# A GEGLU feed-forward kernel: up of the first pair of f tiles by seven products too, together with the second pair

## Chip, cores, metric

One core of one Trainium2 chip. The metric is the device time of one execution in microseconds (us). Most executions of one kernel agree to within 0.3%, and all runs quoted here count as fast runs; differences of a few tenths of a per cent are therefore read from ratios with a 95% interval, not from single times.

## The reference

```python
def reference(x, w_gate, w_up, w_down):
    return (_gelu(x @ w_gate) * (x @ w_up)) @ w_down
# x 1 x 2048 x 1024, w_gate and w_up 1024 x 3584, w_down 3584 x 1024, all bf16
```

The 3584 columns of w_gate and w_up are 28 "f tiles" of 128. A pair is two f tiles of both gate and up. The rows of x are worked in two halves of 1024, each of two blocks of 512.

## The kernel before

Nearly every matrix product is done by seven block products in place of eight. For a pair, the four 512 x 128 blocks of a weight are combined into left operands s1, s2, s3, s4 and a22, and the blocks of x into right operands t1, t2, t3, t4 and b22. Two of the seven products use blocks as they are ("direct", bf16), five use prepared operands (f32). A product is four matmuls of 512 columns. The sums are made by three engines: s1, s2, s4 by GpSimd (POOL), t1 to t4 and some s3 by VectorE (DVE), a22 and b22 by ScalarE (ACT).

The chain of dependences matters for all that follows: s2 needs s1, s4 needs s2, t2 needs t1, t4 needs t2; t1 and t3 need the second block of x. The code shown here and below is cut (`...`) and in places drawn together; the comments are added.

```python
def t_sum(name, c0=0, c1=KH):                      # right operands
    ...
    in0, in1 = {
        "t1": lambda: (b(0, 1), b(0, 0)),
        "t2": lambda: (b(1, 1), tsum["t1"].bitcast(F32)[:, c0:c1, :]),
        "t3": lambda: (b(1, 1), b(0, 1)),
        "t4": lambda: (b(1, 0), tsum["t2"].bitcast(F32)[:, c0:c1, :]),
    }[name]()
    dve(nc.vector.tensor_tensor(out=t, in0=in0, in1=in1, op=ALU.subtract))

def s_sum(h, pair, j, name, on_dve=False, staged=True):   # left operands
    ...
    if name == "s1":   tt(a(1, 0), a(1, 1), ALU.add)
    elif name == "s2": tt(s1, a(0, 0), ALU.subtract)      # s1 from above
    elif name == "s3": tt(a(0, 0), a(1, 0), ALU.subtract)
    elif name == "s4": tt(a(0, 1), s2, ALU.subtract)      # s2 from above
    else:              act(nc.scalar.copy(out=t, in_=a(1, 1)))
```

Only the first pair of the program is not done so, since at the start there is no time to prepare operands: it is 64 direct matmuls, during which the rest is loaded and the second pair's operands are made.

```python
def first_pair_units(hT):
    held = (VB, RB)
    transpose_x0(0)
    warm(RB[1], TB // 2)
    part(held, 0, 0, KPQ, js=(0,))      # gate, first block of x
    transpose_x0(1)
    part(held, 0, 0, KPQ, js=(1,))      # up
    part(held, 0, KPQ, KD)              # gate and up, the rest of the first block
    t_sum("t1", 0, KH // 2)
    t_sum("t1", KH // 2, KH)
    ...
    held = (QB, PB)
    part(held, 1, 0, KH)                # gate and up, second block of x
    t_sum("t2")
    t_sum("b22")
    t_sum("t3", 0, KH // 2)
    ...
    for name in ("s1", "s2", "s4"):     # operands of the second pair
        for j in range(2):
            s_sum(0, 1, j, name)
```

The loads ahead of it bring only the first 256 columns (two f tiles) of the first 512 of gate and up. The other 256 of both follow behind the second block of x.

```python
FA = 2 * P
load_x0(0, sp, 0, 2)
load_x0(0, act, 2, TSB)
load_w(first, 0, 0, 2, sp, 0, FA)
load_x0(1, act)
load_w(first, 1, 0, 2, sp, 0, FA)
load_w(first, 0, 2, 5, act, 0, FA)
load_w(first, 1, 2, 5, sp, 0, FA)
...                                     # transposed x of the first block, weights 5 to 8
for k0, k1 in ((0, 2), (2, KH), (KH, KD)):
    load_xT(xT, 0, 1, k0, k1)           # second block of x
for j in range(2):
    load_w(first, j, 0, KD, sp, FA, FG) # late columns of gate and up
```

Of the kernel before, what the change touches and what calls it, by code (L numbers as in the profile page):

```python
# [34 lines left out]
def kernel(  # L35
# [8 lines left out]
    nc = tc.nc  # L44
# [77 lines left out]
    def act(inst):  # L122
        return on("act", inst)

    def dve(inst):
        return on("dve", inst)
# [55 lines left out]
        new_x(tb)  # L182
    new_chunk((0, 0))

    FA = 2 * P
    first = (0, 0)
    load_x0(0, sp, 0, 2)
    load_x0(0, act, 2, TSB)
    load_w(first, 0, 0, 2, sp, 0, FA)
    load_x0(1, act)  # L190
    load_w(first, 1, 0, 2, sp, 0, FA)
    load_w(first, 0, 2, 5, act, 0, FA)
    load_w(first, 1, 2, 5, sp, 0, FA)
    ident = const_pool.tile([P, P], BF16, name="ident")
    make_identity(nc, ident[:])

# [13 lines left out]

    for i in range(NWARM):
        warm(i)

    load_xT(xT, 0, 0, KH, KH + 1)
    behind_transpose = last_on["sp"]
    load_xT(xT, 0, 0, KH + 1, KH + 2)
    for j in range(2):
        load_w(first, j, 5, KD, act, 0, FA)
        tc.add_manual_dep(
            last_on["act"].ins,  # L220
            behind_transpose.ins.name,
            SCHED_DEP,
            reason="engine order",
        )
    act(nc.scalar.preload_act_table(ACT.Gelu_apprx_tanh))
    load_xT(xT, 0, 0, KH + 2, KD)
    for k0, k1 in ((0, 2), (2, KH), (KH, KD)):
        load_xT(xT, 0, 1, k0, k1)
    for j in range(2):
        load_w(first, j, 0, KD, sp, FA, FG)  # L230
    new_chunk((0, 1))
    for j in range(2):
        load_w((0, 1), j, 0, KD)


    tsum = {}
# [35 lines left out]

    g_ctr = [0]

    def gelu(ps, last=False):

        if last:
            g_sb = o_pool.tile([P, TB], F32, name="o_sb")[:]
        else:
            e0 = 4 * CH + (g_ctr[0] % 4) * 2 * TB  # L280
            g_ctr[0] += 1
            g_sb = w_mem[:, e0 : e0 + 2 * TB].bitcast(F32)
        act(nc.scalar.activation(out=g_sb, in_=ps[:], func=ACT.Gelu_apprx_tanh))  # L283
        return g_sb

    def mult(hT, g_sb, ps, fc, tb):
        dve(
# [5 lines left out]
            )  # L293
        )

    def unit_out(hT, bset, fi, tb):
        mult(hT, gelu(banks[bset[0]]), banks[bset[1]], fi, tb)

    def transpose_x0(q):

        parts = [(2 * q, 0, 4), (2 * q + 1, 0, 4)]
        if q == 0:
            parts = [(0, 0, 2), (0, 2, 4), (1, 0, 4)]
        for n, (kd, ts0, ts1) in enumerate(parts):
            tp = banks[(PB + QB)[(2 * q + n) % 4]][:].bitcast(BF16)
            for ts in range(ts0, ts1):
                pe(
                    nc.tensor.transpose(  # L308
                        tp[:, ts * P : (ts + 1) * P],
                        xs0[:, ts, kd * P : (kd + 1) * P],  # L310
                        ident[:],
                    )
                )
            cols = slice(ts0 * P, ts1 * P)
            if q == 0 or n == 0:
                dve(nc.vector.tensor_copy(out=xT[0][:, kd, cols], in_=tp[:, cols]))
            else:
                act(nc.scalar.copy(out=xT[0][:, kd, cols], in_=tp[:, cols]))

    def part(held, tb, k0, k1, us=(0, 1), js=(0, 1)):  # L320
        for kd in range(k0, k1):
            for j in js:
                for u in us:
                    mm_gu(banks[held[u][j]], chunks[first][j], u, tb, kd)

    def first_pair_units(hT):

        held = (VB, RB)
        transpose_x0(0)
        warm(RB[1], TB // 2)  # L330
        part(held, 0, 0, KPQ, js=(0,))
        transpose_x0(1)
        part(held, 0, 0, KPQ, js=(1,))
        part(held, 0, KPQ, KD)
        t_sum("t1", 0, KH // 2)
        t_sum("t1", KH // 2, KH)
        for u in range(2):
            unit_out(hT, held[u], u, 0)
        held = (QB, PB)
        part(held, 1, 0, KH)  # L340
        t_sum("t2")
        t_sum("b22")
        t_sum("t3", 0, KH // 2)
        part(held, 1, KH, KD, (0,))
        unit_out(hT, held[0], 0, 1)
        t_sum("t3", KH // 2, KH)
        part(held, 1, KH, KD, (1,))
        unit_out(hT, held[1], 1, 1)
        for j in range(2):
            s_sum(0, 1, j, "s3", True, False)  # L350
        for name in ("s1", "s2", "s4"):
            for j in range(2):
                s_sum(0, 1, j, name)


    ssum = {}
# [1 line left out]

    def block(key, j, i, kh):
        fi = 2 * (key[2] % PPG) + i  # L360
        w_sb = chunks[(key[0], key[2] // PPG)][j]
        return w_sb[:, half(kh), fi * P : (fi + 1) * P]

    def s_sum(h, pair, j, name, on_dve=False, staged=True):
        key = (h, "p", pair)

        def a(i, kh):
            return block(key, j, i, kh)

        if on_dve and staged and name in ("s1", "s2", "s3"):  # L370

            if j == 0:
                first_s[name] = wd_pool.tile([P, WDT, D], BF16, name="wd_sb")
            t = first_s[name][:, j, :].bitcast(F32R)
        else:
            s0 = (2 * S_NAMES.index(name) + j) * KH * P
            t = s_mem[:, s0 : s0 + KH * P]
        t = t.rearrange("p (a b) -> p a b", b=P)
        ssum[(h, pair, j, name)] = t

        def tt(in0, in1, op):
            if on_dve:
                dve(nc.vector.tensor_tensor(out=t, in0=in0, in1=in1, op=op))
            else:
                pool(nc.gpsimd.tensor_tensor(out=t, in0=in0, in1=in1, op=op))  # L385

        if name == "s1":
            tt(a(1, 0), a(1, 1), ALU.add)
        elif name == "s2":
            s1 = ssum[(h, pair, j, "s1")].bitcast(F32)  # L390
            tt(s1, a(0, 0), ALU.subtract)
        elif name == "s3":
            tt(a(0, 0), a(1, 0), ALU.subtract)
        elif name == "s4":
            s2 = ssum[(h, pair, j, "s2")].bitcast(F32)
            tt(a(0, 1), s2, ALU.subtract)
        else:
            act(nc.scalar.copy(out=t, in_=a(1, 1)))  # L398
# [6 lines left out]
    def pair_quads(hT, h, pair, nxt, then):  # L405
# [49 lines left out]
        def do_m5(j):  # L455
            mm(V_[j], j, s(j, "s1"), tsum["t1"], True)
            m5[j] = m_pool.tile([P, TB], F32, name=f"m5_{j}")
            act(nc.scalar.copy(out=m5[j][:], in_=banks[V_[j]][:]))  # L458
            if not eager:
                prep(j, "s1")  # L460

        def do_m6(j):
            mm(QB[j], j, s(j, "s2"), tsum["t2"], False)
# [3 lines left out]
            mm(P_[j], j, block(key, j, 0, 0), b11, True)  # L467
            act(nc.scalar.copy(out=banks[QB[j]][:], in_=banks[P_[j]][:]))  # L468
        behind = len(pending) > 0
        eager = not behind and "m2" in then  # L470
        if behind:

            pending.pop()()
# [1 line left out]
        if behind:  # L475
            if nxt is None:
                m2()
                done("m2")
            else:
                pending.append(m2)  # L480
            order = (do_m6, 0), (do_m6, 1), (do_m5, 0), (do_m5, 1)
        elif eager:
            m2()
            done("m2")
            order = (do_m5, 0), (do_m5, 1), (do_m6, 0), (do_m6, 1)
        else:
            pending.append(m2)
            order = (do_m5, 0), (do_m6, 0), (do_m6, 1), (do_m5, 1)
# [3 lines left out]
                done("m6")  # L492
        for j in range(2):
            add_m5(QB[j], QB[j])
            if not eager:
                prep(j, "s2")
        done("m5")
        if eager:
            pool_behind_dve()
            for name in ("s1", "s2"):  # L500
                for j in range(2):
                    prep(j, name)
        for j in range(2):
            mm(RB[j], j, s(j, "s3"), tsum["t3"], False)
            add_m5(V_[j], RB[j])
# [343 lines left out]
    for h in range(NH):  # L849
        hT = hT_pool.tile([P, KF, SH], BF16, name="hT")  # L850
        first_pair = 0
        if h == 0:
            first_pair_units(hT)
            first_pair = 1
            xs = [(tb, kd) for tb in (1, 0) for kd in range(KD)]
            new_x(1)
            stage_load(0)
            stage_load(1)
        for pair in range(first_pair, NPAIR):
            then = {}  # L860
            if pair % PPG == 0 and (pair // PPG + 1) * PPG < NPAIR:
                key = (h, pair // PPG + 1)

                if key not in chunks:
                    new_chunk(key)
                    for j, at in enumerate(("m2 of last", "m3")):
                        then[at] = [lambda j=j: load_w(key, j, 0, KD, act)]
            if h == 0 and pair < PPG:
                then = {
                    "m2": [lambda j=j: s_sum(0, pair, j, "a22") for j in range(2)]  # L870
                    + [lambda: t_sum("t4", 0, KH // 2)],
                    "m5": [lambda: t_sum("t4", KH // 2, KH)],
                }
            if h == 0 and pair >= PPG:

                n = [min(4 * (pair - PPG + d), NSTEP) for d in range(3)]
                steps = [lambda k=k: stage_step(k) for k in range(n[0], n[1])]
                new = range((n[1] + 2) // 3, (n[2] + 2) // 3)

# [53 lines left out]
        if h + 1 < NH:  # L933
# [1 line left out]
            new_x(0)  # L935

            def x_fill():
                for k0, k1 in ((0, 2), (2, KH), (KH, KD)):
                    src = x_rows(k0, k1)
                    sp(nc.sync.dma_start(out=xT[0][:, k0:k1, :], in_=src))  # L940

# [66 lines left out]
```

## Time and profile before

| | before |
|---|---|
| median of the runs beside the change | 540.12 us (539.45 to 541.44, 6 runs) |
| TensorE (PE) busy | 99% of the span |
| waits of PE | one, 0.8 us, at the very start |
| third pair begins on PE | 32.09 us |
| late columns of up landed (POOL's first sum of them) | 19.07 us |

The kernel is bound by PE from beginning to end, so what matters is whether PE ever stands still. The mark used throughout is the moment at which the third pair begins on PE: from there on both kernels do the same, and what is behind at this mark is behind at the end, give or take a wait of up to 1.1 us just behind it. The table of stretches shows what the other engines do meanwhile. Its columns are: stretch in us, its length, then busy us and instructions of PE, weight loads, DVE, ACT and POOL, the granted clock of PE, the mean busy share of the DMA engines and what they moved in GB/s.

```profile
18.00:23.00 5.00, 4.95 (x24) 2.36 (x24) 5.00 (x5) 2.79 (x6) 4.62 (x4) 1.00 1.10 343
23.00:28.00 5.00, 5.00 (x24) 3.90 (x23) 5.00 (x6) 3.17 (x6) 5.00 (x3) 1.00 0.85 296
```

From 18 to 28 us DVE and POOL are both busy nearly all the time, that is working or standing in each other's way, and the DMA still moves about 300 GB/s. PE is fully busy nevertheless: until 22.71 us it does direct products, which need none of what DVE and POOL are making, and by then the first prepared operands are there.

### The profile page before, as it was taken

How to read it: one execution, taken by the hardware profiler on the slowest of the kernel's cores; microseconds unless marked ns; L12 is line 12 of the kernel's file. 1: busy time of each engine (PE TensorE's matmuls, PEld its weight loads, DVE VectorE, ACT ScalarE, POOL GpSimd, SP SyncE). 2: the span in 40 equal slices, each digit the busy share in tenths (PEclk: the TensorE clock that was granted, in tenths of full speed). 3: DMA queues.
4: the chain of work that ended last, by engine and by line, in shares of the span. 5: the costliest groups of instructions: out<-in, count | busy, mean ns of one | idle time of the engine just before them, and what ended most of it. 6: DMA issues, size and time to landing. Idle time of an engine off the chain costs nothing.

```text
span 537.8 us, 7068 instructions
## 1 busy us (share of the span) xinstructions
PE 531.9 (99%) x2348; PEld 377.9 (70%) x2384; DVE 363.9 (68%) x475; ACT 263.2 (49%) x446; POOL 244.3 (45%) x212
## 2 busy tenths in 40 slices
PE   9999999999999999999999999999999999999997
PEld 4577777667776686777776677777777766866866
DVE  2988767788775997989674334444454469969961
ACT  2555555555555329117465555555555551452270
POOL 0689877777776000000066766667777730000000
PEclk9999999999999999999999999999999999999999
DMA  9946876685816977779940404042222447677846
GB/s 215 328 120 194 213 242 209 221 266 187 292 60 207 356 237 265 230 271 318 321 161 1 156 1 158 24 134 71 86 78 80 157 143 282 228 230 252 292 146 207
DMA packets 92419, 102.70 MB, mean 191 GB/s; under 512 B 18656, under 2 KB 67296, under 8 KB 92384
## 3 DMA queue, kind: packets, MB, share of 16 engines
q1 hardware_dynamic: 69584, 80.30, 45.8%
q10 hardware_dynamic: 22800, 21.96, 13.1%
q8 instruction: 19, 0.31, 0.3%
q14 instruction: 16, 0.13, 0.1%
HBM read 85.98 MB, written 12.58 MB: 183 GB/s over the span
## 4 chain that ended last, share of the span: by engine, by line
PE 99%; issue 0%; ACT 0%; ACTq 0%
PE bank L413 63%; PE bank L700 33%; PE bank L264 3%; PE bank L202 1%; PE bank L308 0%; ACT o_sb L753 0%; ACT bank L468 0%; ACTq L753 0%; ACTq L468 0%
## 5 line engine op out<-in xcount | busy, mean ns | idle before, releaser
L413 PE MATMUL bank<-t_mem,s_mem 128*128 128x512 f32 x1056 | 249.4, 394 | 0.0
L413 PEld LDWEIGHTS bank<-t_mem,s_mem 128*128 128x128 f32 x1056 | 198.1, 188 | 43.8 <-ACT bank L464 0.3
L385 POOL TENSOR_TENSOR s_mem<-w_mem 128x512 fp32r<-128x512 bf16 x102 | 119.4, 1192 | 190.3 <-DMA w_mem<-in_w_up_dram 103.1
L700 PE MATMUL bank<-t_mem,s_mem 128*128 128x512 f32 x544 | 127.1, 392 | 0.0
L288 DVE TENSOR_TENSOR hT<-w_mem,bank 128x512 bf16<-128x512 f32 x104 | 71.2, 686 | 80.5 <-PE bank L413 46.2
L700 PEld LDWEIGHTS bank<-t_mem,s_mem 128*128 128x128 f32 x544 | 102.2, 188 | 22.1
L436 DVE TENSOR_TENSOR bank<-bank,m 128x512 f32<-128x512 f32 x108 | 69.8, 694 | 44.6 <-ACT m L458 43.3
L413 PE MATMUL bank<-xT,w_mem 128*128 128x512 bf16 x405 | 96.5, 380 | 1.4
L283 ACT ACTIVATE w_mem<-bank 128x512 f32<-128x512 f32 x104 | 61.8, 596 | 53.1 <-DVE bank L436 35.6
L413 PEld LDWEIGHTS <-w_mem 128*128 128x128 bf16 x432 | 40.2, 98 | 51.6 <-issue 6.8
L385 POOL TENSOR_TENSOR s_mem<-w_mem,s_mem 128x512 fp32r<-128x512 bf16 x52 | 66.4, 1301 | 0.0
L605 DVE TENSOR_TENSOR t_mem<-w_mem 128x1024 fp32r<-128x1024 bf16 x56 | 65.6, 1218 | 0.0
L385 POOL TENSOR_TENSOR s_mem<-s_mem,w_mem 128x512 fp32r<-128x512 f32 x52 | 61.3, 1199 | 0.0
L464 ACT COPY bank<-bank 128x512 f32<-128x512 f32 x54 | 30.8, 570 | 38.9 <-PE bank L413 38.9
L398 ACT CAST s_mem<-w_mem 128x512 fp32r<-128x512 bf16 x54 | 33.1, 615 | 30.6 <-PE bank L413 29.1
L675 DVE TENSOR_TENSOR s_mem<-hT 128x512 fp32r<-128x512 bf16 x52 | 34.2, 686 | 10.0 <-PE bank L700 9.4
L458 ACT COPY m<-bank 128x512 f32<-128x512 f32 x54 | 31.7, 587 | 17.5 <-PE bank L413 17.5
L700 PEld LDWEIGHTS <-hT 128*128 128x128 bf16 x224 | 21.3, 98 | 26.6 <-issue 2.1
L468 ACT COPY bank<-bank 128x512 f32<-128x512 f32 x54 | 30.7, 570 | 12.7 <-PE bank L413 12.7
L753 ACT CAST o_sb<-bank 128x512 bf16<-128x512 f32 x28 | 15.4, 586 | 39.6 <-PE bank L700 39.6
L630 DVE TENSOR_TENSOR o_sb<-wd_sb,o_sb 128x512 fp32r<-128x512 bf16 x28 | 31.5, 1126 | 0.5
L602 ACT CAST t_mem<-w_mem 128x1024 fp32r<-128x1024 bf16 x28 | 26.9, 1048 | 0.0
(42 smaller groups left out, 237.9 us busy)
## 6 DMA issues: line engine op xcount, KB each, us to landing
t_mem<-t_dram SPq DMA_DIRECT2D x56, 512.0 KB, 5.3
w_mem<-in_w_gate_dram ACTq DMA_DIRECT2D x10, 1024.0 KB, 5.1
w_mem<-in_w_up_dram ACTq DMA_DIRECT2D x10, 1024.0 KB, 5.4
wd_sb<-in_w_down_dram SPq DMA_DIRECT2D x28, 256.0 KB, 4.2
t_dram<-o_sb SPq DMA_DIRECT2D x28, 256.0 KB, 2.4
wd_sb<-in_w_down_dram SPq DMA_DIRECT2D x12, 512.0 KB, 7.8
w_mem<-in_w_down_dram SPq DMA_DIRECT2D x4, 1024.0 KB, 6.3
w_mem<-in_w_down_dram SPq DMA_DIRECT2D x8, 512.0 KB, 8.6
```

What stands on the lines that cost most here:

```text
L283: act(nc.scalar.activation(out=g_sb, in_=ps[:], func=ACT.Gelu_apprx_tanh))
L288: nc.vector.tensor_tensor(out=hT[:, fc, tb * TB : (tb + 1) * TB], in0=g_sb, in1=ps[:], op=ALU.mult,)
L385: pool(nc.gpsimd.tensor_tensor(out=t, in0=in0, in1=in1, op=op))
L398: act(nc.scalar.copy(out=t, in_=a(1, 1)))
L413: nc.tensor.matmul(banks[bank][:], lhsT=lhs[:, c, :], rhs=rhs[:, c, :], start=start and c == 0, stop=c == KH - 1, skip_group_check=True,)
L436: nc.vector.tensor_tensor(out=banks[dst][:], in0=banks[src][:], in1=m5[j][:], op=ALU.add)
L458: act(nc.scalar.copy(out=m5[j][:], in_=banks[V_[j]][:]))
L464: act(nc.scalar.copy(out=banks[RB[j]][:], in_=banks[QB[j]][:]))
L605: dve(nc.vector.tensor_tensor(out=t, in0=in0, in1=in1, op=ALU.subtract))
L630: dve(nc.vector.tensor_tensor(out=t, in0=in0, in1=in1, op=ALU.subtract))
L675: dve(nc.vector.tensor_tensor(out=t, in0=in0, in1=in1, op=op))
L700: nc.tensor.matmul(banks[bset[u]][:], lhsT=lhs(i, u), rhs=rhs(i), start=start and i == 0, stop=stop and i == NS - 1, skip_group_check=True,)
```

## The change

The intent: the up half of the first pair is also done by seven products, which saves 4 of its 32 matmuls. It is done in one run with the second pair, as three "units": gate of the second pair, up of the first, up of the second. Gate of the first pair stays direct.

The pairs of the first chunk become f tiles (0, 2) and (1, 3). The direct gate then needs tiles 0 and 2, so all of gate's columns have to come early, in rows of 1024 bytes; of up only two tiles are early, and its late columns are needed by both up units. They are queued behind the second block of x. The head's loads are also cut into smaller pieces, spread over two queues. Cut to its core:

```diff
-    FA = 2 * P
-    load_x0(0, sp, 0, 2)
-    load_x0(0, act, 2, TSB)
-    load_w(first, 0, 0, 2, sp, 0, FA)
     ... (the rest of the loads shown above)
+    def head_w(j, k0, k1, queue):
+        load_w(first, j, k0, k1, queue, 0, (FG, 2 * P)[j])   # gate whole, up half
+    head(head_x, sp, 0, 0)
+    head(head_x, act, 0, 2)
+    head(head_w, sp, 0, 0, 1)
+    head(head_w, act, 0, 1, 2)
     ... (nine more pieces of x, gate, up and transposed x)
+    head(head_w, act, 1, KH, KD)
+    head(head_xT, sp, 0, KH + 2, KD)
+    head(head_w, act, 0, KH + 2, KD)
+    for k0, k1 in ((0, 2), (2, KH), (KH, KD)):
+        head(head_xT, sp, 1, k0, k1)
+    load_w(first, 1, 0, KD, sp, 2 * P, FG)                   # late columns of up
-    def first_pair_units(hT):
     ...
+    def first_chunk(hT):
+        units = ((1, 0), (0, 1), (1, 1))                     # (pair, 0 gate / 1 up)
     ...
+        gate(0, KD - 2, KD)
+        s(0, "a22")
     ...
+        for name in ("s1", "s2", "s4"):
+            s(0, name)
+        t_sum("t1", 0, KH // 2)
+        t_sum("t1", KH // 2, KH)
+        for name in ("s1", "s2", "s4"):
+            for i in each[1:]:
+                s(i, name)
+        for i in each:
+            on_x0(i, KD - 2, KD)
+            unit_out(i, banks[P_[i]], 0, 0)
+        gate(1, 0, KD)
+        t_sum("t2")
+        t_sum("b22")
+        for i in each[1:]:
+            t_sum("t3", (i - 1) * KH // 2, i * KH // 2)
+            s(i, "s3", True)
+        gate_out(1)
+        for i in each:
+            product(i, P_[i], "s1", "t1", True)
+            copy(m5[i], P_[i])
     ...
+        for i in each:
+            product(i, Q_[i], "s2", "t2")
+            copy(banks[R_[i]], Q_[i])
+        add(banks[Q_[0]], Q_[0], 0)
+        t_sum("t4", 0, KH // 2)
     ... (s3, s4, a22 with t3, b22, t4 in the same way)
 def block(key, j, i, kh):
     fi = 2 * (key[2] % PPG) + i
+    if (key[0], key[2] // PPG) == first:
+        fi = key[2] + 2 * i
 ...
             def x_fill():
-                for k0, k1 in ((0, 2), (2, KH), (KH, KD)):
+                for k0, k1 in ((0, KD),):
```

The marked cuts also hide the removal of a special order for the second pair (`eager`) that is no longer needed.

## The prediction

> **What bounds the kernel now.** I read the page first, then the matmul groups by form, the waits of the tensor engine, and the timeline of the first 45 us, because the change touches only the first chunk of weights (f tiles 0 to 3) and the loads ahead of it.
>
> ```profile
> PE 531.9 (99%) x2348; PEld 377.9 (70%) x2384; DVE 363.9 (68%) x475; ACT 263.2 (49%) x446; POOL 244.3 (45%) x212
> PE 99%; issue 0%; ACT 0%; ACTq 0%
> ```
>
> The tensor engine is busy 99% of the span and is 99% of the chain that ended last. The waits of PE hold a single entry:
>
> ```profile
> PE bank L202 <- PEq L992: 0.8, 1, 0.8
> ```
>
> So in this kernel one matmul saved is one matmul's pace saved, and any wait put on PE is added to the end in full, since nothing behind it has slack to take it up. Two rules of pace come from the timeline of PE:
>
> ```profile
> 6.49 13.11 PE L264 MATMUL bank<-xT,w_mem 128*128 128x512 bf16 x59
> 19.43 3.63 PE L413 MATMUL bank<-xT,w_mem 128*128 128x512 bf16 x15
> 22.71 9.54 PE L413 MATMUL bank<-t_mem,s_mem 128*128 128x512 f32 x40
> 32.09 1.90 PE L413 MATMUL bank<-xT,w_mem 128*128 128x512 bf16 x7
> 33.64 9.44 PE L413 MATMUL bank<-t_mem,s_mem 128*128 128x512 f32 x40
> 42.93 3.63 PE L413 MATMUL bank<-xT,w_mem 128*128 128x512 bf16 x15
> ```
>
> The reader is to see the starts: 6.49 to 19.43 us is 60 bf16 matmuls of the first pair (one record missing), 0.216 us each. From 33.64 to 42.93 us is 40 f32 ones, 9.29 us; single records inside it stand 0.2275 us apart, apart from the first. The chunk ends, for this argument, where the third pair begins: 32.09 us. That is the mark to beat.
>
> **What the Trainium skill says.** "TensorE: Matmul & The Clock Gate", section "Back-to-back issue gap", gives N/2.4 + 2.5 ns when warm, 215.8 ns for N = 512; the trace agrees for bf16 (0.216). The f32 step of 0.2275 is a little more. "SBUF — State Buffer", section "SBUF: two separate sides", says that VectorE with two SBUF inputs and GpSimd share a port pair held as "an exclusive lock, not a bandwidth split"; the loser waits for the whole instruction. The trace agrees to a few hundredths of a us:
>
> ```profile
> 15.40 2.29 DVE L259 TENSOR_TENSOR t_mem<-xT,t_mem 128x2048 fp32r<-128x2048 bf16 x1
> 17.60 2.18 DVE L259 TENSOR_TENSOR t_mem<-xT 128x1024 fp32r<-128x1024 bf16 x1
> 20.30 1.58 DVE L259 TENSOR_TENSOR t_mem<-xT 128x1024 fp32r<-128x1024 bf16 x1
> ...
> 17.34 1.35 POOL L385 TENSOR_TENSOR s_mem<-w_mem 128x512 fp32r<-128x512 bf16 x1 [16.04 <-DMA w_mem<-in_w_gate_dram]
> 19.07 1.72 POOL L385 TENSOR_TENSOR s_mem<-w_mem 128x512 fp32r<-128x512 bf16 x1 [0.38 <-DMA w_mem<-in_w_up_dram]
> 20.76 3.71 POOL L385 TENSOR_TENSOR s_mem<-s_mem,w_mem 128x512 fp32r<-128x512 f32 x2
> ```
>
> POOL's first sum ends at 18.69; the DVE difference issued at 17.60 ends at 19.78, 1.09 us later; POOL's second ends at 20.79, 1.01 us later; DVE's next ends at 21.88, 1.09 later. They alternate. So I take 1.05 us of the port for a POOL sum, 1.09 for a DVE difference of 1024 columns, 2.29 for one of 2048, and 0.52 for a DVE weight sum of 512 (two took 22.40 to 25.02 with two POOL turns between). "DMA: Bandwidth & Descriptors", section "Latency and other measured facts", gives 261 GB/s for DMA transposes; here the stretch from 8 to 13 us, nearly all transposes, moved 232, while 18 to 23 us (rows of 1024 bytes) moved 343.
>
> **The change part by part.**
>
> 1. Matmuls. Up of the first pair goes from 32 direct matmuls to 28 (two direct products of 4, five of prepared operands of 4). Over the program the instruction order has 24 fewer bf16 matmuls and 20 more f32 ones: 24 x 0.216 - 20 x 0.2275 = 5.18 - 4.55 = 0.63 us off. If nothing waits, the time is 539.97 - 0.63 = 539.3. Everything else decides by how much this is overdrawn.
>
> 2. Order on PE. Before: 64 direct matmuls, then the second pair (16 direct, 40 prepared). After: 40 direct on the first block of x, 16 gate on the second block, then 60 prepared in the order s1, s2, s3, s4, a22, three units each. With PE starting as before, the prepared ones start 8 x 0.216 earlier than 19.43: 17.7 us. Each product of 4 takes 0.91: s1 of the units at 17.7, 18.6, 19.5; s2 at 20.4, 21.3, 22.3; end at 31.4 without waits (32.09 - 31.4 is the 0.63 again, give or take rounding). Before, the prepared products began at 22.71, five us later.
>
> 3. Loads. Units two and three are the up halves, pairs of f tiles (0,2) and (1,3), so both need the late columns of up. These are queued behind x of the second block. In the kernel before, POOL's second sum tells when the late up landed: 19.07. By then 4.0 MB had landed: x 0.5, early weights 1.0, transposed x 1.5, late gate and late up 1.0. After, the same 4.0 MB lie in front of the same landing, because all of gate now comes first. Gate in rows of 1024 bytes and fewer stretches of bare transposes save perhaps half a us: late up at 18.5 (estimate; 17.8 to 19.2). X of the second block, last at 15.06 before, has 0.5 MB more ahead of it: about 16.4.
>
> 4. The port. POOL needs four sums after 18.5 (s1, s1, s2, s2) before PE's sixth product, which without waits would start at 22.3. Alone they would take 4 x 1.05 and end at 22.7. But DVE holds the same port in turn: t1 (two of 1.15), two products off PSUM (0.68 each), t2 (2.29), t3 in halves (1.09), s3 of the units (0.52). POOL also makes s1, s2, s4 of the gate unit from about 12.3 on, when gate has landed, and these take turns with t1, whose inputs land at 13.3 and 14.5. Running it by hand: t1 is done at 17.2, s4 of the gate unit at 18.3, the first s1 of up at 19.5 (or behind t2, at 20.8), t2 at 21.7, the second s1 at 22.8, half of t3 23.9, s2 25.0, s3 25.5, the last s2 26.5. The sixth product then starts at 26.6 and not 22.3. Nine products follow, 8.2 us, after its own 0.9: end at 35.7, if DVE's adds and t4 keep up; they come out within 1 us of the limit on either side. Against 32.09 this is 3.6 later, up to 4.9 where t4 and the adds bind too.
>
> 5. The rest. Two sums of the following pair are made behind t4 as before; the single load of transposed x for the second half replaces three far ahead of use. I give both 0.
>
> The head may lose 0 to 0.5 us on late gate or up rows (needed near 10.7 and 12.2, landing near 10.5 and 12), but that is hidden: the end of the chunk hangs on the port chain. Sum: 539.97 + 3.6 to 4.9 by my central run; a run in which all lands as early as before gives about +1.5. I take +3.8: **543.8 us**.
>
> **The rivals.** *First: no new wait.* The author placed the loads and sums with care, and the saving of 0.63 would show: 539.3. For it speaks that PE waits nowhere now, in a head just as tight. Against it: the prepared products come 5 us earlier than before while the late columns they rest on come no more than half a us earlier or so. *Second: the wait is only that for late up* (POOL and DVE don't collide much): the last s2 at 23 to 24, +0.5 to +1.5, so 540.5 to 541.5. Against it speaks the alternation in the lines above. *Third: the head stalls too or PE's clock drops in the waits.* The waits come in pieces of about a us; the clock column shows 9 in all slices. A drop to half pace over some us would add 1 to 2: 545 to 546. *Fourth: DVE alone binds* through t2, t3, the adds and t4 (9.6 us of its own work after t2 starts near 18): +1 to +4.9, about what the port gives.
>
> **Range and chances.** None of these is near 2% (10.8 us). The low end allows for the second rival: 540.2. The high end takes the port with DVE's adds: 545.6. First rival about 1 in 8. Faster by 2% has no mechanism: 0.002; slower by 2% would need 12 us of wait: 0.013.
>
> **What would show it.** In the profile after: x24 fewer bf16 and x20 more f32 matmuls on PE; waits of PE on POOL's sums (s_mem) or gaps before the prepared products between 18 and 28 us, of 3 to 5 us in all; POOL's first sum of up starting at 18 to 19.5 us behind a DMA of up; sums of 1.5 to 2.3 us in turns with DVE; the third pair beginning near 35.5 instead of 32.09. If POOL's last s2 is done by 22.3 us, or PE has no gap there, I am wrong, and the time is 539.3. If late up lands before 17 us, step 3 is wrong; if sums and differences overlap freely, step 4 is.

## The result, and the profile after

A ratio is the mean time of one kernel's fast runs over that of the other's of the same rounds, so it isn't quite the ratio of the medians.

| | before | after |
|---|---|---|
| median | 540.12 us | 545.75 us (545.2 to 547.78, 6 runs) |
| ratio | | 1.0107 [1.0088, 1.0127] |
| third pair begins on PE (profiled run) | 32.09 us | 39.64 us |
| PE's prepared products begin | 22.71 us | 19.81 us |
| t4 complete | 29.5 us | 34.1 us |

The change costs about 5.6 us. It is the same at a threshold of 2%, but clearly not a gain. The profiled execution of the changed kernel was the slowest of its six (547.78 us), which matters below. Two lines of the page:

```profile
PEclk9889999999999999999999999999999999999999
PE 94%; DMA 2%; POOL 2%; issue 1%; SPq 0%; ACT 0%; POOLq 0%; ACTq 0%
```

The chain that ended last was PE for 99% before; now DMA and POOL have 2% each of it. The clock line shows 8 in the second and third slice (13.6 us each). The waits of PE (us in total, times, longest), without the 0.8 us at the start that it had before:

```profile
PE bank L386 <- POOL s_mem L519: 2.6, 2, 1.9
PE bank L271 <- DMA xT<-in_x_dram: 1.7, 3, 0.8
PE bank L359 <- DMA w_mem<-in_w_up_dram: 0.2, 1, 0.2
```

Before, that one was the only wait: now PE also waits for POOL's sums and for loads. The timeline of PE (start, duration, instruction, in brackets the idle time before it and what ended it) shows where:

```profile
18.27 1.89 PE L271 MATMUL bank<-xT,w_mem 128*128 128x512 bf16 x8 [0.64 <-DMA xT<-in_x_dram]
19.81 1.28 PE L386 MATMUL bank<-t_mem,s_mem 128*128 128x512 f32 x4
22.97 1.35 PE L386 MATMUL bank<-t_mem,s_mem 128*128 128x512 f32 x4 [1.88 <-POOL s_mem L519]
25.06 12.92 PE L386 MATMUL bank<-t_mem,s_mem 128*128 128x512 f32 x44 [0.74 <-POOL s_mem L519]
...
39.64 1.90 PE L547 MATMUL bank<-xT,w_mem 128*128 128x512 bf16 x7
```

One product is done, then PE waits 1.88 us for s1 of the second unit and 0.74 for that of the third. After 25.06 the list shows 44 matmuls without a gap, yet 12.92 us for them; at 0.2275 us each they would take 10. The table of stretches tells why:

```profile
18.00:23.00 5.00, 2.85 (x13) 1.47 (x12) 5.00 (x5) 3.63 (x7) 2.29 (x2) 1.00 1.08 328
23.00:28.00 5.00, 4.25 (x11) 3.00 (x12) 5.00 (x4) 1.41 (x3) 5.00 (x3) 0.59 1.08 365
28.00:33.00 5.00, 5.00 (x17) 3.95 (x17) 4.36 (x6) 2.50 (x5) 4.40 (x3) 0.73 0.07 23
```

PE does 13, 11 and 17 matmuls where it did 24 in each of these stretches before, and its granted clock falls to 0.59 and 0.73: the clock records have half speed from 23.89 to 30.71 us. In that time the matmuls stand 427 ns apart. So two causes lie on top of each other in this trace, waits for sums and a slow clock, and the trace alone can't say which of them carries the 5.6 us. DVE meanwhile is as full as before, and POOL's first sum of up waits for a load. Its timeline, with DVE's between:

```profile
12.94 1.15 POOL L519 TENSOR_TENSOR s_mem<-w_mem 128x512 fp32r<-128x512 bf16 x1 [11.63 <-DMA w_mem<-in_w_gate_dram]
...
20.71 4.29 POOL L519 TENSOR_TENSOR s_mem<-w_mem 128x512 fp32r<-128x512 bf16 x2 [3.29 <-DMA w_mem<-in_w_up_dram]
24.97 3.72 POOL L519 TENSOR_TENSOR s_mem<-s_mem,w_mem 128x512 fp32r<-128x512 f32 x2
```

```profile
21.83 2.17 DVE L266 TENSOR_TENSOR t_mem<-xT 128x1024 fp32r<-128x1024 bf16 x1
23.92 1.64 DVE L517 TENSOR_TENSOR s_mem<-w_mem 128x512 fp32r<-128x512 bf16 x1
```

A POOL sum with nobody beside it takes 1.15 us. The four of up take about 2 us each, and each difference of DVE beside them about 1 us more than alone (1.21 and 0.68, as an experiment below shows): they take turns. The last s2 is done at 28.69, and after it DVE has all of t4 still to make. The landings themselves stand in the trace too: the last piece of x of the second block landed at 18.23 us (15.06 before), the late columns of up at 20.64 (19.01 before).

### The profile page after: what moved, and what is told of

Read it like the earlier page. It is cut to its first block, busy times and chain, and to the rows that moved or that the text cites. A ratio compares the mean times of both kernels' runs of the same rounds, so it can differ in the third digit from the quotient of the medians.

```text
span 545.7 us, 7082 instructions
## 1 busy us (share of the span) xinstructions
PE 535.1 (98%) x2345; PEld 380.4 (70%) x2380; DVE 367.6 (67%) x479; ACT 264.7 (49%) x449; POOL 248.5 (46%) x215
## 3 DMA queue, kind: packets, MB, share of 16 engines
q10 hardware_dynamic: 22832, 22.42, 13.6%
## 4 chain that ended last, share of the span: by engine, by line
PE 94%; DMA 2%; POOL 2%; issue 1%; SPq 0%; ACT 0%; POOLq 0%; ACTq 0%
PE bank L547 60%; PE bank L822 32%; PE bank L386 3%; POOL s_mem L519 2%; DMA w_mem<-in_w_gate_dram 1%; DMA w_mem<-in_w_up_dram 1%; SPq L166 0%; ACT o_sb L875 0%; SPq L160 0%; POOLq L519 0%; ACTq L875 0%
## 5 line engine op out<-in xcount | busy, mean ns | idle before, releaser
L547 PE MATMUL bank<-t_mem,s_mem 128*128 128x512 f32 x1016 | 239.8, 394 | 0.0
L547 PEld LDWEIGHTS bank<-t_mem,s_mem 128*128 128x128 f32 x1016 | 190.8, 188 | 41.8
L822 PE MATMUL bank<-t_mem,s_mem 128*128 128x512 f32 x544 | 127.4, 393 | 0.0
L301 DVE TENSOR_TENSOR hT<-w_mem,bank 128x512 bf16<-128x512 f32 x100 | 68.6, 686 | 79.8 <-PE bank L547 45.6
L822 PEld LDWEIGHTS bank<-t_mem,s_mem 128*128 128x128 f32 x544 | 102.1, 188 | 22.5 <-DVE s_mem L797 0.4
L570 DVE TENSOR_TENSOR bank<-bank,m 128x512 f32<-128x512 f32 x104 | 67.3, 694 | 46.5 <-ACT m L592 45.0
L547 PE MATMUL bank<-xT,w_mem 128*128 128x512 bf16 x390 | 92.9, 380 | 1.4
L283 ACT ACTIVATE w_mem<-bank 128x512 f32<-128x512 f32 x100 | 59.5, 597 | 44.8 <-DVE bank L570 32.7
L547 PEld LDWEIGHTS <-w_mem 128*128 128x128 bf16 x416 | 38.6, 98 | 49.7 <-issue 6.8
L519 POOL TENSOR_TENSOR s_mem<-w_mem,s_mem 128x512 fp32r<-128x512 bf16 x53 | 68.4, 1314 | 0.1
L532 ACT CAST s_mem<-w_mem 128x512 fp32r<-128x512 bf16 x54 | 33.2, 615 | 33.8 <-PE bank L547 29.5
L597 ACT COPY bank<-bank 128x512 f32<-128x512 f32 x52 | 29.6, 570 | 38.2 <-PE bank L547 38.2
L822 PEld LDWEIGHTS <-hT 128*128 128x128 bf16 x224 | 21.3, 98 | 26.6 <-issue 2.1
L592 ACT COPY m<-bank 128x512 f32<-128x512 f32 x52 | 30.6, 589 | 17.0 <-PE bank L547 17.0
L601 ACT COPY bank<-bank 128x512 f32<-128x512 f32 x52 | 29.7, 570 | 11.7 <-PE bank L547 11.7
L752 DVE TENSOR_TENSOR o_sb<-wd_sb,o_sb 128x512 fp32r<-128x512 bf16 x28 | 29.5, 1052 | 0.5
```

Of the source, the lines that this page charges most:

```text
L283: act(nc.scalar.activation(out=g_sb, in_=ps[:], func=ACT.Gelu_apprx_tanh))
L301: nc.vector.tensor_tensor(out=hT[:, fc, tb * TB : (tb + 1) * TB], in0=g_sb, in1=ps[:], op=ALU.mult,)
L519: pool(nc.gpsimd.tensor_tensor(out=t, in0=in0, in1=in1, op=op))
L547: nc.tensor.matmul(banks[bank][:], lhsT=lhs[:, c, :], rhs=rhs[:, c, :], start=start and c == 0, stop=c == KH - 1, skip_group_check=True,)
L570: nc.vector.tensor_tensor(out=banks[dst][:], in0=banks[src][:], in1=m5[j][:], op=ALU.add)
L592: act(nc.scalar.copy(out=m5[j][:], in_=banks[V_[j]][:]))
```

## The experiments

My theory: the operands of the prepared products can't exist when PE gets to them, because the sums of POOL and of DVE share one port and start only when the late loads land; the products were to come 5 us earlier (they came 2.9 us earlier in the trace) and the operands didn't. Rivals: the slow clock is the cause; the landing of up's late columns alone is; the rearranged loads are. Each kernel ran in rounds beside the kernel before. The experiments ran in three groups of four, each group on one chip; the kernel before had medians of 540.23, 540.19 and 540.23 us beside them.

### The same kernel again

No edit. It separates the slow clock of a single execution from what belongs to the kernel.

> The changed kernel, unaltered, for a second trace and its spread. Expected 545 to 546.5 us. The first trace had four kinds of loss before the third pair: waits for loads in the head (2.6 us), waits for POOL's sums of up (3.1 us), half clock from 23.9 to 30.7 us (about 2.7 us), against 0.63 saved. If these are regular, they show again, and the third pair begins at 37.5 to 40 us (32.1 in the kernel before). If the stretch of slow loads at 7 to 12 us was a chance of that one execution, the head's waits are gone here and the time still stays near 545.5, because POOL's chain sets the end.

Measured: 546.92 us (545.46 to 547.13), ratio 1.0113 [1.0097, 1.013]; third pair at 39.27 us; half clock again in the profiled run (mean 0.994). The result repeats. But of the first six executions two had a mean clock of 1.000 and took 545.39 and 546.11 us, amid the four others, whose clock was 0.994 to 0.997 and whose times were 545.2 to 547.78. So the slow clock comes in some executions only, and the loss is there without it. (The 2.6 us of waits for loads in the expectation are too many: the waits shown above add up to 1.9.)

### PE kept busy in the waits

Matmuls on constants, into a bank that the next product overwrites, fill the two waits.

```diff
         for i in each:
+            for _ in range((0, 7, 4)[i]):
+                warm(P_[i])
             product(i, P_[i], "s1", "t1", True)
```

> Dummy matmuls fill the two waits for POOL's sums: 7 before s1 of the second unit, 4 before s1 of the third, into the bank that the next product clears. Theory (the half clock is the tensor engine's answer to its waits): clock 1.0 throughout, no matmuls of 427 ns between 20 and 35 us, time 0.5 to 2.7 us below the changed kernel of the same rounds (some of its executions had no half clock or a short one). Rival (the clock falls for other reasons, or POOL's chain is later anyway and hides it): no gain, or half clock all the same.

Measured: 545.95 us (545.35 to 546.27), ratio 1.0103 [1.0088, 1.0118], clock 1.0 throughout. The timeline of PE:

```profile
28.29 7.59 PE L386 MATMUL bank<-t_mem,s_mem 128*128 128x512 f32 x32 [0.67 <-POOL s_mem L521]
...
37.53 1.90 PE L549 MATMUL bank<-xT,w_mem 128*128 128x512 bf16 x7
39.86 7.52 PE L549 MATMUL bank<-t_mem,s_mem 128*128 128x512 f32 x32 [0.42 <-DVE hT L301]
```

At full clock PE gets to the sixth product sooner and waits there for POOL's s2; it goes on at 28.29 us, ends 1.7 to 2.1 us sooner than in the two traces with the slow clock, and then waits 0.42 us for DVE inside the third pair. The median is 0.97 us below that of the repeat beside it, which the theory's 0.5 to 2.7 includes, but 0.2 above that of the first six executions, and the intervals of the ratios overlap. So the slow clock is real and may be up to 2 us of the slowest executions, but for the most part it fills time in which PE would have waited for operands: at full clock 5.7 us are still lost. It is not the cause.

### No sums of up on POOL (wrong result on purpose)

The two up units use gate's s1, s2 and s4 in place of their own, so that POOL has six sums fewer. The loads, DVE's work and PE's matmuls stay.

```diff
         for name in ("s1", "s2", "s4"):
             for i in each[1:]:
-                s(i, name)
+                pair, j = units[i]
+                ssum[(0, pair, j, name)] = ssum[(0, 1, 0, name)]
```

> Wrong result on purpose: units two and three (up) use the gate unit's s1, s2 and s4 in place of their own, so POOL makes three sums in the first chunk and not nine, and these products wait neither for POOL nor for the late up columns (s3 and a22 of up still do). Theory (POOL's sums behind the late landing set the end): PE has no wait for POOL, third pair begins at 33 to 35 us, time 540.5 to 542.5. Rival (head and the vector engine's t2, t3, adds and t4 set it anyway): 544 or more.

Measured: 541.09 us (540.84 to 542.04), ratio 1.0018 [1.0003, 1.0033]. PE and DVE:

```profile
19.06 12.17 PE L386 MATMUL bank<-t_mem,s_mem 128*128 128x512 f32 x52
...
32.88 1.90 PE L548 MATMUL bank<-xT,w_mem 128*128 128x512 bf16 x7
35.40 9.33 PE L548 MATMUL bank<-t_mem,s_mem 128*128 128x512 f32 x40 [0.61 <-DVE hT L301]
```

```profile
21.14 1.21 DVE L266 TENSOR_TENSOR t_mem<-xT 128x1024 fp32r<-128x1024 bf16 x1
22.28 0.68 DVE L518 TENSOR_TENSOR s_mem<-w_mem 128x512 fp32r<-128x512 bf16 x1
```

All waits between the products are gone, and the time falls by 5.8 us against the unchanged repeat on the same chip, by 4.9 against keep_warm, which like it ran at full clock. DVE's instructions take 1.21 and 0.68 us where they took 2.17 and 1.64, and t4 is complete at 28.8 us in place of 34. So POOL's sums of up carry the loss. But this edit takes away two things at once: the work on the port, and the wait for the late columns, which these sums need. The next two take them apart.

### The up units on columns that are there early (wrong result on purpose)

```diff
         if (key[0], key[2] // PPG) == first:
-            fi = key[2] + 2 * i
+            fi = key[2] + 2 * i if j == 0 else (key[2] + i) % 2
```

Up's operands are made from f tiles 0 and 1, which land early; all work stays.

> Wrong result on purpose: the up units take all their blocks from the early columns, so nothing waits for the late ones; POOL makes all its nine sums, and these still share with the vector engine. Theory A (the late landing is what hurts): near no_up_sums, 541 to 542.5. Theory B (the turns with the vector engine hurt even with columns early): POOL runs from 13 us without a pause, six sums and three with turns of about 1.05 plus the differences, last s2 of up near 22 to 24 us, 543 to 544.5.

Measured: 546.8 us (546.46 to 547.0), ratio 1.012 [1.0105, 1.0135], clock 1.0. No gain, and above both ranges: it is even 0.85 us slower than keep_warm, which ran at full clock too. POOL, then PE:

```profile
18.84 4.31 POOL L519 TENSOR_TENSOR s_mem<-w_mem 128x512 fp32r<-128x512 bf16 x2
23.11 3.71 POOL L519 TENSOR_TENSOR s_mem<-s_mem,w_mem 128x512 fp32r<-128x512 f32 x2
```

```profile
23.20 3.30 PE L386 MATMUL bank<-t_mem,s_mem 128*128 128x512 f32 x12 [1.94 <-POOL s_mem L519]
26.88 4.85 PE L386 MATMUL bank<-t_mem,s_mem 128*128 128x512 f32 x20 [0.38 <-POOL s_mem L519]
32.35 2.08 PE L386 MATMUL bank<-t_mem,s_mem 128*128 128x512 f32 x8 [0.62 <-DVE bank L409]
...
37.56 1.90 PE L547 MATMUL bank<-xT,w_mem 128*128 128x512 bf16 x7
40.55 6.63 PE L547 MATMUL bank<-t_mem,s_mem 128*128 128x512 f32 x28 [1.10 <-DVE hT L301]
```

POOL waits for no load between its sums and is through with s2 at 26.8 us, 1.3 to 1.9 sooner than in the three traces with up's own columns. PE still waits 2.3 us for its sums. And in exchange POOL's turns delay DVE's t2 (3.17 us where it took 2.28), so PE now also waits 0.62 and 0.15 for DVE's adds and 1.10 for DVE's product in the third pair, and t4 isn't complete before 33.9. The landing of the late columns isn't what the end hangs on. The second block of x, from which DVE's chain starts, landed late in this run as well (17.48 us); no run moved that alone.

### The sums of up on DVE

s1 and s2 of the up units go from POOL to DVE, behind t2; s4 stays with POOL. The result is correct.

```diff
-        for name in ("s1", "s2", "s4"):
-            for i in each[1:]:
-                s(i, name)
 ...
         t_sum("t2")
+        for name in ("s1", "s2"):
+            for i in each[1:]:
+                s(i, name, True)
+        for i in each[1:]:
+            s(i, "s4")
```

> The up units' s1 and s2 (four sums) are made on the vector engine behind t2 and not on POOL; s4 stays on POOL. Correct result. No_up_sums and early_cols say that the turns of POOL and the vector engine on one port set the end, not the late landing. If it is the turns, four turns of 1.05 us and the alternation go for four vector sums of 0.55 to 0.7, all in one queue: s1 of the second unit ready near 22, s2 of the third near 24, PE's third pair at 35 to 36.5 and the time 542 to 543.5. If the sheer amount of work on the vector engine binds, no gain: 545 to 547.

Measured: 545.91 us (545.53 to 546.52), ratio 1.0105 [1.009, 1.012]; third pair at 37.65 us. The second alternative came true, no gain. The waits of PE:

```profile
PE bank L271 <- DMA xT<-in_x_dram: 2.0, 2, 1.2
PE bank L386 <- DVE t_mem L266: 1.3, 1, 1.3
PE bank L549 <- DVE hT L301: 1.1, 1, 1.1
PE bank L386 <- DVE s_mem L519: 1.0, 1, 1.0
```

The wait for POOL (2.6 us in the first trace) has become waits for DVE, 2.3 us before the third pair and 1.1 in it. (In this trace x of the second block landed at 18.94, some 1.2 us later than in keep_warm, which also puts the start of the prepared products off to 20.52.) It seems that each of the two engines can be relieved only at the other's cost: what they have to do after the second block of x is there stays nearly the same.

### Gate's unit ahead

PE does both s1 and s2 of the gate unit, whose operands are early, before it comes to up.

```diff
-        for i in each:
-            product(i, P_[i], "s1", "t1", True)
-            copy(m5[i], P_[i])
 ...
+        s1_product(0)
+        s2_product(0)
+        s1_product(1)
+        s1_product(2)
 ...
+        s2_product(1)
+        s2_product(2)
```

> Only PE's order: the gate unit's s2 product directly behind its s1 product, so that it lies in the wait for POOL's first sum of up. If POOL's last sums set the end anyway, no gain (within 0.5 us of the changed kernel, 546 to 547) and the wait shows up at a later product; if the first wait counts by itself, 0.9 less.

Measured: 545.45 us (544.89 to 546.36), ratio 1.0101 [1.0085, 1.0118], clock 1.0; third pair at 36.67 us, about a microsecond sooner than in keep_warm. But in this trace x of the second block also landed 0.9 us sooner (16.91 against 17.78) and late up 1.0 (19.33 against 20.36), so that the sooner mark isn't shown to come from the order. The interval of the ratio covers the change itself. PE still waits 2.2 us for POOL and 1.0 for t2. With both edits together (this order and the sums of up on DVE):

> Sums_on_dve and gate_first together on the changed kernel. If the vector engine's own chain (t4 done at 32.4 to 34 us in all of these) sets the end, no better than 545; if the two add, 543.5 to 544.5.

Measured: 545.58 us (545.15 to 546.15), ratio 1.0099 [1.0084, 1.0114]; third pair again at 36.67, then a wait of 1.10 us for DVE. PE now waits 2.8 us for t_mem, the operands that DVE makes of x. Neither order nor division of the work gets the time back.

### The late columns of gate late as well: a miss

The changed computation with the loads of the kernel before (shown above in full), so gate's late columns come behind x too.

> Loads as in the kernel before: the early 256 columns of gate and up first, the late columns of both behind x of the second block; the computation is that of the changed kernel. Direct products need only early columns, so the head should have no wait (2.6 us of them go), x of block two lands at 15.1 again and not 17.5, late gate at 17.3, late up at 19. Theory (POOL's chain sets the end, and its start is set by t1 and by the gate sums): the gate sums start at 17.3 and not 13, before nine sums in a row, so the end comes not earlier: 544.5 to 547. Rival (loads and head waits set the end): 542 to 543.

Measured: 555.23 us (555.04 to 555.46), ratio 1.0277 [1.0262, 1.0292]. My premise was wrong: the direct gate of the first pair works on f tiles 0 and 2, and tile 2 is among the late columns. PE stood still for it, 12.6 us in one wait for gate's columns.

The failed run shows something all the same. POOL was through with all its sums of up by 30.6 us, before PE's first prepared product at 31.98, and from there the 60 prepared matmuls take 13.8 us (to 45.79) with no wait: 0.230 us each, PE's own pace for them. Once their operands are there, nothing holds the products up; what they lack in the changed kernel is a lead for the operands.

### The loads alone

The kernel before with the changed kernel's loads, in two steps. In the second, gate's early part is 256 columns as before, so that only the order and the small pieces differ from the kernel before.

```diff
 (loads_only: the kernel before, its loads replaced by those of the change)
 (loads_early: the same, and)
     def head_w(j, k0, k1, queue):
-        load_w(first, j, k0, k1, queue, 0, (FG, 2 * P)[j])
+        load_w(first, j, k0, k1, queue, 0, 2 * P)
 ...
-    load_w(first, 1, 0, KD, sp, 2 * P, FG)
+    for j in range(2):
+        load_w(first, j, 0, KD, sp, 2 * P, FG)
```

> The kernel before with the loads of the changed one: all of gate in wide rows first, late up behind x of block two. If mixing wide gate rows with the transposes slows the head by itself, PE waits there (some 1 to 2.5 us), and the time is 541 to 543; if the head's waits come from the changed order of work on PE, 540.0 to 540.5.

> The kernel before with the pieces, queues and order of the changed kernel's loads, but gate only in its early 256 columns there, its late columns behind x of block two as before. Loads_only took 2.4 us more than before. If the 512 KB of gate that came forward (and their wide rows) are the cause, this is 540.0 to 540.6 and the third pair begins at 32.1 to 32.5 us. If the new order and pieces (transposes issued some 1.4 us later on the sync queue) are the cause, 541.5 to 542.6.

Measured: loads_only 542.57 us (542.5 to 542.65), ratio 1.0042 [1.0028, 1.0057], third pair at 34.72; loads_early 541.52 us (540.93 to 541.87), ratio 1.0023 [1.0006, 1.0039], third pair at 33.48. So the loads by themselves cost the old computation about 2.3 us (0.42%), perhaps half of it by order and pieces (the two intervals overlap). In the three stretches of 5 us from 3 to 18 us PE is busy 4.38, 4.47 and 4.75 us in loads_only, where it was busy 5.00, 4.95 and 5.00 before.

The cost of the loads and that of the computation can't be added up: both push the same moment, and the later one sets it.

### Gate whole, but in narrow rows: confounded

> As loads_only (all of gate first), but every piece of gate in two transfers of 256 columns, so that rows are 512 bytes and not 1024. If wide rows beside transposes are what slows the engines of the transfers, 540.3 to 541.3; if it is the amount that has to land first, 542 to 543.5 (five more issues can add a little).

loads_only, with each piece of gate as two transfers of 256 columns. Measured: 545.51 us (544.95 to 545.54), ratio 1.0095 [1.008, 1.011]; third pair at 37.05. The waits of PE show why this says nothing on the width of rows:

```profile
PE bank L272 <- ACT xT L326: 2.5, 1, 2.5
```

The added transfers are issued from ACT's queue, and ACT's copy of the transposed x stood behind them, so that PE waited for the copy. Whether wide rows beside transposes are slow to land stays open.

### The changed computation with loads and pairs as before

Neighbouring f tiles form a pair again, gate of the first pair is tiles 0 and 1, and both late halves come behind x. The unit of the first pair's up (early columns) goes first, the direct products of the other two units behind the direct gate. The result is correct.

```diff
-        units = ((1, 0), (0, 1), (1, 1))
+        units = ((0, 1), (1, 0), (1, 1))
 ...
-                    mm_gu(banks[G_[u]], chunks[first][0], 2 * u, tb, kd)
+                    mm_gu(banks[G_[u]], chunks[first][0], u, tb, kd)
 ...
         gate_out(1)
+        product(0, P_[0], "s1", "t1", True)
+        for i in each[1:]:
+            on_x0(i, 0, KH)
+            copy(banks[Q_[i]], P_[i])
+            on_x0(i, KH, KD)
 ...
+        product(0, Q_[0], "s2", "t2")
```

> The changed computation with the loads of the kernel before. Pairs are adjacent f tiles again (0,1),(2,3), so up of the first pair needs only early columns: it is the first unit, with the gate of the first pair direct; the second pair's direct products come behind gate's second block. Same 116 products in the chunk. Correct result. Four products fewer, but PE has only 24 direct products until x of block two lands (11.5 to 15.1 us) and waits there some 3 us; the sums of late columns start at 17.3 and 19.1 as before. I expect the third pair at 33 to 34.5 us (32.1 before), 541 to 542.5. If the waits were only those of the changed loads, 539.3 to 539.8.

Measured: 544.81 us (544.59 to 545.06), ratio 1.0084 [1.0069, 1.0099]; third pair at 36.30, both later than I expected. The waits of PE:

```profile
PE bank L277 <- DMA xT<-in_x_dram: 1.7, 3, 1.0
PE bank L365 <- ACT bank L411: 1.5, 3, 0.7
PE bank L557 <- DVE hT L307: 0.8, 1, 0.8
```

This is the lowest measured median of the versions with up by seven products and a correct result (its interval overlaps that of gate_first), and still 4.6 us behind the kernel before. The waits for POOL are gone, but the direct products that I had moved into the gap brought a wait of their own that I hadn't foreseen: the first direct product of a unit must be copied by ACT into a second bank before PE may add the second one, and a unit by itself leaves PE nothing to do meanwhile. And with fewer direct matmuls in the head, PE gets to the second block of x before it has landed. No version that I tried beats the kernel before.

## Why the prediction was right and wrong

**Step 1, the matmuls: right.** The instruction order has 24 bf16 matmuls fewer and 20 f32 more, and f32 products without waits ran at nearly the predicted pace (13.8 us for 60 in late_both, 12.0 us for the 52 from 19.06 to 31.07 in no_up_sums). So the 0.63 us follow from counts and paces, but no run shows them as time, under what follows.

**Step 2, the start of the prepared products: too early.** I had 17.7 us; in the traces with these loads it was 18.48 to 20.52, in that of the result 19.81. The waits in the head, which I put at "0 to 0.5 us" and called hidden, came to 1.9 us there. No_up_sums shows what they are worth alone: with every wait for sums gone, the third pair begins at 32.88 in place of the 31.4 of the text.

**Step 3, the loads: mis-sized.** In three traces (the result, the repeat, keep_warm) late up landed at 20.64, 19.61 and 20.36 us and not at 18.5, later than the 19.01 of before and not sooner. The last of x of the second block landed at 18.23, 17.62 and 17.78 and not at 16.4. The saving of "perhaps half a us" doesn't show. From 3 to 18 us the DMA moved 241 GB/s in each of these traces, on the mean of the three stretches, against 263 before; my estimate from that is 0.3 MB less by 18 us, or about 0.9 us at the 343 GB/s of the next stretch. Gate whole was to be there at 12.3 and landed at 12.26 to 13.40. Why these loads are slower is open.

**Step 4, the port: the mechanism was right, two of its terms failed.** POOL and DVE alternate as described, and where no turn of the other stands between, the instructions fall back to their short durations.

The first term is the start of POOL's chain, which it had from step 3. Since up landed later, its first sum stood behind the whole of t2 and ended at 22.4 to 22.9, not at 19.5 or 20.8; the lag stayed. The last s2 was to be done at 26.5 and was at 28.1 to 28.7; the sixth product started at 28.29 (keep_warm) and not at 26.6. Counted from there the prediction's own sum gives the measured one: 28.29 and the ten products behind it (9.2 us) is 37.5, where keep_warm begins its third pair. So this term was mis-sized by 1.7 us.

The second term is the clause that I had left as a condition, "if DVE's adds and t4 keep up". Early_cols tells: there the columns are early, POOL's four sums end at 20.0, 23.2, 25.3 and 26.8, close to the 19.5, 22.8, 25.0 and 26.5 of my run by hand, and still the third pair begins at 37.56 and not at 35.7. The sixth product starts at 26.88 there, and the ten products take 10.7 us in place of 9.2: the difference lies at the two waits for DVE's adds, which stand in DVE's queue behind t4's halves. So the adds don't keep up; t4 itself was complete 0.7 us before its first product (34.59). How late DVE's whole chain runs shows in t4: it is complete at 32.4 to 34.1 us in the versions whose loads are those of the change and whose up sums are their own (after, again, keep_warm, early_cols, gate_first, sums_on_dve), against 28.8 without POOL's sums of up. DVE's own chain, the fourth rival, lies on the heels of the port chain, and relieving either shows the other.

A rough estimate from these durations says why: without POOL's sums of up DVE needs 13.1 us from the second half of t1 to the end of t4 (15.65 to 28.76 in no_up_sums), in the changed kernel 17.8 (16.33 to 34.1). The difference of 4.7 us is less than the six turns of 1.05 us (6.3) that POOL takes. Some of these turns fall in DVE's waits or beside its adds, which took 0.69 to 0.70 us with POOL at work and 0.68 to 0.69 without.

One reading in the prediction is off besides: "two took 22.40 to 25.02 with two POOL turns between" leaves 0.26 us for each weight sum at 1.05 a turn, not 0.52; alone one took 0.68 (no_up_sums). The effect on the sum is some tenths of a us.

**Step 5, the rest taken as 0: short by up to 1.1 us.** In the traces at full clock DVE's backlog is carried over the mark: the third pair's first prepared product waits for DVE's multiplication to free its bank (0.42 in keep_warm, 0.61 in no_up_sums, 1.10 in early_cols). In the two traces with the slow clock there is no such wait.

**The sum.** I predicted 3.8 us; 5.6 were measured. In the run at full clock: third pair at 37.53, 5.4 us behind before, and 0.4 of wait behind it, 5.8 together, beside 5.7 between the medians. Against the +3.6 of the central run that is 1.8 from the later end of the port and load chain, and the 0.4 of step 5.

**The rivals.** The first, no new wait, is refuted by the trace. The second, the landing alone, is refuted by early_cols. The third came true in the trace (waits in the head, half the clock for 6.8 us), and its 545 to 546 is the measured time; but keep_warm takes as long at full clock, so that the figure fits by luck and not by its reason. The fourth is the other half of the cause.

**Where the gain went.** The four matmuls were saved. But in the kernel before, the first pair's direct products were what hid the loads and the making of operands. The change took 0.6 us of work out of PE (by count), moved the operands' use about 3 us forward (22.71 to 19.81; by plan 5) and had POOL make nine sums in the first chunk in place of six, on a port that was already full. The operands come later, and PE waits for them.

What stays open: how the 2.3 us of loads_only divide between wide rows and their place in the queues (the test of it was confounded); how much of t4's lateness is the later landing of x, from which DVE's chain starts (old_loads has it at 15.52 us, but with new waits of its own); the single load of x for the second half, which wasn't run by itself, though it lies far ahead of its use; and why the clock falls in some executions only.

## What to carry to other kernels

Work that is slow to start is cover for what has to be prepared: before a product is replaced by a cheaper one that needs prepared operands, ask when the operands can exist at the earliest, and not how long the products take. Where two engines share a port, add up the work of both from the moment their common input lands to the last operand; moving a sum from one to the other, or its input earlier, changed only the name in the list of waits here. When a trace shows a slow clock beside waits, fill the waits with idle matmuls in a test kernel before blaming the clock: here it ran at full clock and took the same time.

## What the Trainium skill lacked or had wrong

- "TensorE: Matmul & The Clock Gate", section "What's actually happening", has PE fall to half clock after an idle window of about 3.4 us. Here the half clock lasted 6.8 us (23.89 to 30.71) and followed waits of which none was longer than 1.9 us, with PE busy for 2.85 of the 5 us from 18 to 23. The section "A second HAM failure mode: psum-queue depth-cycling" does speak of short and frequent idle times, but names another cause for them; here they were waits for operands, and only some executions of the same kernel had the drop; early_cols, with a wait of 1.94 us at the same place, kept full clock. Matmuls of 512 columns stood 427 ns apart in it.
- The same page, section "Back-to-back issue gap": it has the formula of the prediction (216 ns for 512 columns) for an isolated matmul only, and about 131 ns for 512 columns in a real stream of weight loads and matmuls, which the prediction left out. Here the stream of bf16 matmuls, each with its weight load, ran at 0.216 us, so that the formula agrees and the 131 ns don't. For f32 operands no step is given; 60 of them ran at 0.230 us each, 0.2275 within a product.
- "SBUF — State Buffer", section "SBUF: two separate sides": the exclusive lock agrees. That two engines with work in hand take turns instruction by instruction, and what a turn costs, isn't there: a POOL sum of 512 columns 1.15 us alone and about 2 in turns, a DVE difference of 1024 columns 1.21 alone and 2.17 in turns.
- "DMA: Bandwidth & Descriptors", section "Latency and other measured facts", has 261 GB/s for transposes with a non-contiguous middle dimension and about 350 to 400 for contiguous ones. Transposes mixed with plain loads from two queues moved 227 to 253 GB/s from 8 to 13 us in three traces of the changed kernel's loads (the result, the repeat, keep_warm) and 232 before; no page has a figure for the mixture.
